# Where the overflow table of the first expert mixture is built: beside the experts, or inside a loop that runs when rows overflow

## The chip, the cores and the metric

The kernel runs on one core of one Trainium2 chip. The metric is device time in microseconds (us) for one execution. [...]

## The reference

The program computes an attention without softmax, then two mixtures of experts, over N = 4608 rows of 512 numbers.

```python
def _attn_ref(q, k, v, g_norm):
    kv = np.einsum('bhsd,bhse->bhde', k, v)
    out = np.einsum('bhsd,bhde->bhse', q, kv)
    rms = np.sqrt(np.mean(out * out, axis=-1, keepdims=True) + 1e-06)
    return out / rms * g_norm

def _moe_ref(x, w_gate, w_output_gate, w1, w2):        # first mixture, 8 experts
    logits = x @ w_gate
    e_idx = np.argmax(logits, axis=1)
    ...
    for e in range(E):
        mask = e_idx == e
        h = np.maximum(x[mask] @ w1[e], 0.0)           # 512 -> 1024
        ye = h @ w2[e]                                 # 1024 -> 512
        out[mask] = gate_w[mask, None] * eom[mask, e, None] * ye
```

The first mixture sends each row to the expert with its largest logit, with no limit on how many rows an expert gets. The second mixture assigns rows greedily with a limit of 576 rows for each expert, and computes the same kind of feed-forward with its own weights.

## The kernel before

Products are done in three passes of a high and a low part (names ending in h and l), so that a result has nearly full fp32 precision. Names: `ph` is the first product's PSUM, `hh` and `hl` the high and low part of its relu, `py` the second product's PSUM, `y` the scaled result, `raw` a weight as loaded, `w1h`, `w1l`, `w2h`, `w2l` its parts, `xg` gathered rows, `sg` their scale, `pt` transposes.

The first mixture's rows are sorted into experts by tables of indices. `experts()` runs over the eight experts, p = 0 to 7, in an order sorted by size, with room for CAPS[p] rows each (672, 704, 672, 640, 608, 608, 576, 544). An expert is eight blocks of `ffn1` (PE products `ph`, ACT `hh`, DVE `hl`), with the splitting of its second weights in blocks 0 to 3 and gathers of the next expert's rows (POOL's indirect DMAs into `xg` and `sg`) in blocks 4 to 7. Then come the rest of the gathers. Behind these, at what is called the boundary here, stands `next(ovf, None)`: one step of `overflow_tables()`. After that the second products of this expert are made tile by tile (PE `py`, ACT `y`, POOL scatters into `x_rows`, DVE logits of the second mixture, scattered by POOL into `l_rows`), beside the splitting of the next expert's first weights (ACT, and POOL's DMAs `w1l`) and the transposes of its gathered rows.

Rows that find no room in their expert go into an overflow table `ovt` in DRAM, in groups of 128. `overflow_tables()` is a generator. In its first step, after expert 0, it fills `ovt` with N by a DMA (L842), counts the groups into `left`, and computes for each row the place in the table (`ri`) and the row's number (`ti`). Each of the six later steps, after experts 1 to 6, issues six scatters of `ti` into `ovt`, each after a small memset of `gap`: 36 in all. After the experts, `left` is read (L1091) and a loop (L1092) runs `spare()` for each group, which reads `ovt`, and gathers, multiplies and scatters. `left` is zero where no row overflows.

The order of PE, DVE, ACT and POOL is written by hand: instructions stand in their lists as the Python code issues them (`manual_schedule`). Nearly all operations pass through one helper, so that they carry its line, L94.

Of the kernel before, what the change touches and what calls it, by code (L numbers as in the profile page):

```python
# [29 lines left out]
N = B * S  # L30
DM = H * D
E = 8
FF = 1024
NT = N // 128
# [21 lines left out]
NOV = 36  # L56
# [43 lines left out]
def moe_chain_kernel(ctx, tc, q, k, v, g_norm, wg1, wog1, w1a, w2a, wg2, w1b, w2b, out, dbg=None):  # L100
    nc = tc.nc
    V = Meter(nc.vector, 150, 1.04)
    A = Meter(nc.scalar, 40, 0.9)
    G = Meter(nc.gpsimd, 70, 2.18)
# [3 lines left out]
    def T(pool, shape, dt, name, **kw):  # L108
        return pool.tile(shape, dt, name=name, **kw)
# [3 lines left out]
    def dram(name, shape, dt=F32):  # L113
        return dbg[name] if name in dbg else tc.dram_tile(shape, dt, name=name)
# [40 lines left out]
    def floor_div(dst, src, n):  # L155

        V.tensor_scalar(dst, src, 1.0 / n, 0.5 / n - 0.5, op0=OP.mult, op1=OP.add)
        V.tensor_scalar(dst, dst, MAGIC, MAGIC, op0=OP.add, op1=OP.subtract)
# [16 lines left out]
    rank_k = T(keep, [128, NT], F32, "rank_k")  # L175
    eid_k = T(keep, [128, NT], F32, "eid_k")
    oneh_k = T(keep, [128, NT, E], BF, "oneh_k")
    cacc = T(keep, [128, E], BF, "cacc")
    V.memset(cacc, 0.0)
    code = T(keep, [128, NT], F32, "code")  # L180
# [6 lines left out]
    cap_e = T(keep, [128, E], F32, "cap_e")  # L187
# [33 lines left out]
    with ExitStack() as at:  # L221
# [243 lines left out]
        with tc.manual_schedule(engines={ENG.PE, ENG.Activation, ENG.DVE, ENG.Pool}):  # L465
# [72 lines left out]
            for t in range(NT):  # L538
                feed(2)
                r, i = divmod(t, TR)  # L540
# [63 lines left out]
        with tc.tile_pool(name="fin", bufs=1) as fin:  # L604
# [14 lines left out]
            def places(src):  # L619
# [20 lines left out]
                            op=OP.is_equal)  # L640
# [109 lines left out]
    with ExitStack() as m1:  # L750
        m1p = m1.enter_context(tc.tile_pool(name="m1p", bufs=1))
# [20 lines left out]
        gap1 = T(spp, [128, 1], F32, "gap1")  # L772
# [13 lines left out]
        def run(k_):  # L786
            for s_ in told:
                s_()
            told.clear()
            while pieces and k_:  # L790
                k_ -= 1
                f_, last_ = pieces.pop(0)
                f_()
                if last_:
                    told.append(last_)
# [35 lines left out]


        ovt = dram("ovt", [NOV * 128 + N, 1], I32)
        left = T(m1p, [128, 1], I32, "left")
        et = [T(m1p, [128, NOV + 1], I32, f"et{i}") for i in range(2)]
        sfc = T(m1p, [128, 1], F32, "sfc")

        def overflow_tables():
            ov = m1.enter_context(tc.tile_pool(name="ov", bufs=1))
            fill = T(ov, [128, NOV], I32, "fill")  # L840
            V.memset(fill, N)
            nc.gpsimd.dma_start(ovt[:NOV * 128, :].rearrange("(p c) o -> p (c o)", p=128), fill)  # L842
            ne = T(ov, [128, E], F32, "ne")
            V.tensor_sub(ne, cnt, cap_e)
            V.tensor_scalar(ne, ne, 0.0, 127.0, op0=OP.max, op1=OP.add)
            te = T(ov, [128, E], F32, "te")
            floor_div(te, ne, 128)
            inc = T(ov, [128, E], F32, "inc")
            onef = T(ov, [128, E], F32, "onef")
            V.memset(onef, 1.0)  # L850
            V.tensor_tensor_scan(inc, onef, te, 0.0, op0=OP.mult, op1=OP.add)
            V.tensor_copy(left, inc[:, E - 1:])
            cmp = T(ov, [128, NOV + 1, E], F32, "cmp", tag="cmp")
            V.tensor_tensor(cmp, lane_f[:, :NOV + 1, None].to_broadcast([128, NOV + 1, E]),
                            inc[:, None, :].to_broadcast([128, NOV + 1, E]), op=OP.is_ge)
            etf = T(ov, [128, NOV + 1], F32, "etf")
            V.tensor_reduce(out=etf, in_=cmp, axis=AX.X, op=OP.add)
            V.tensor_scalar(et[0], etf, float(E - 1), None, op0=OP.min)
            V.tensor_sub(inc, inc, te)
            of = T(ov, [128, NT, E], F32, "of", tag="cmp")  # L860
            rel = T(ov, [128, NT], F32, "rel")
            row = T(ov, [128, NT], F32, "row")
            V.tensor_mul(of, oneh_k, cap_e[:, None, :].to_broadcast([128, NT, E]))
            V.tensor_reduce(out=rel, in_=of, axis=AX.X, op=OP.add)
            V.tensor_sub(rel, rank_k, rel)
            V.tensor_mul(of, oneh_k, inc[:, None, :].to_broadcast([128, NT, E]))
            V.tensor_reduce(out=row, in_=of, axis=AX.X, op=OP.add)
            isv = T(ov, [128, NT], F32, "isv")
            V.tensor_scalar(isv, rel, 0.0, None, op0=OP.is_ge)
            V.scalar_tensor_tensor(row, row, 128.0, rel, op0=OP.mult, op1=OP.add)  # L870
            dr = T(ov, [128, NT], F32, "dr")
            V.tensor_scalar(dr, code, float(NOV * 128 - 128), None, op0=OP.add)
            V.tensor_sub(row, row, dr)
            V.tensor_mul(row, row, isv)
            ri = T(ov, [128, NT], I32, "ri")
            V.tensor_add(ri, row, dr)
            ti = T(ov, [128, NT], I32, "ti")
            V.tensor_scalar(ti, code, -128.0, None, op0=OP.add)
            V.tensor_scalar(sfc, pid, float(NST * 128), None, op0=OP.add)
            prev = []  # L880
            for c in range(NT):
                if c % 6 == 0:
                    yield
                G.memset(gap1, 0.0)
                st = G.indirect_dma_start(out=ovt, out_offset=bass.IndirectOffsetOnAxis(ap=ri[:, c:c + 1], axis=0),
                                          in_=ti[:, c:c + 1], in_offset=None)
                for o in prev:
                    tc.declare_no_dep(st.ins, o.ins, reason="each scatter writes rows of its own")
                prev.append(st)

        def spare(row0):
            it = T(spp, [128, 1], I32, "it")
# [83 lines left out]
        def tiles(p):  # L976
            return [min(128, CAPS[p] - t * 128) for t in range(-(-CAPS[p] // 128))]

        def load1(p):

            if p:
                EM[p] = nc.sync.value_load(eix[0:1, p:p + 1], min_val=0, max_val=E - 1)
                w1_load(w1a[bass.ds(EM[p], 1)].rearrange("o d f -> (o d) f"), p)
# [56 lines left out]
            V.memset(ones36, 1.0)  # L1040

        late = later()
        ovf = overflow_tables()

        def experts():
            for p in range(E):
                m = CAPS[p]
                nxt_ = tiles(p + 1) if p + 1 < E else []
                if nxt_:
                    load1(p + 1)  # L1050
                for f in range(FC):
                    mm, relu, low = ffn1(f, m // 2)
                    low()
                    next(late, None)
                    run(L1)
                    if (p, f) == (0, 0):
                        nc.scalar.dma_start(wg2b.rearrange("p e d -> p (e d)"),
                                            bass.AP(tensor=wg2_t.tensor, offset=wg2_t.offset, ap=[[0, 128], [1, E * DM]]))
                    if 0 < m % 128 <= 64:
                        G.tensor_copy(hh[f][:, m:m + m % 128], hl[f][:, m - m % 128:m])  # L1060
                    if f < FC // 2:
                        w2_split(p, f)
                    elif f - FC // 2 < len(nxt_):
                        gather((p + 1) * TS + f - FC // 2)
                for t in range(FC // 2, len(nxt_)):
                    gather((p + 1) * TS + t)
                next(ovf, None)
                own = tiles(p)
                for t in range(max(len(own), len(nxt_))):
                    if nxt_:  # L1070
                        for c in range(2 * t, min(2 * t + 2, KC)):
                            w1_split(p + 1, c)
                    if t < len(nxt_):
                        rows_t(XG[(p + 1) * TS + t][0], t * 128, nxt_[t], gcol2)
                    run(L2 if nxt_ else E)
                    if t < len(own):
                        n, s_ = own[t], p * TS + t
                        py = ffn2_half(t * 128, n) if n <= 64 else ffn2(t * 128, n)
                        if not nxt_ and t == len(own) - 1:
                            run(len(pieces))  # L1080
                        emit_rows(py, XG.pop(s_)[1], idx_s[:, s_:s_ + 1], n, fold=(n <= 64), end=(p == E - 1 and t == len(own) - 1))
                if nxt_:
                    load2(p + 1)
            run(len(pieces))
            run(0)
            for _ in ovf:
                pass

        with tc.manual_schedule(engines={mybir.EngineType[n] for n in "PE,DVE,Activation,Pool".split(",")}):
            experts()  # L1090
        n_left = nc.values_load(left[0:1, 0:1], min_val=0, max_val=NOV)  # L1091
        with tc.For_i(0, n_left, 1) as i:  # L1092
            spare(bass.ds(i * 128, 128))


    rt2 = ctx.enter_context(tc.tile_pool(name="rt2", bufs=1))
# [7 lines left out]
    own = T(rt2, [CG * E, CG, KT], F32, "own")  # L1104
# [259 lines left out]
    cols, rows, row_t = [], [], [0.0]  # L1364
# [176 lines left out]
```

## Time and profile before

| | us |
|---|---|
| median of 3 timed runs (1285.24 to 1288.03) | 1285.33 |
| profiled execution | 1290.72 |
| span of its trace | 1289.1 |
| PE busy | 1122.4 |
| DVE busy | 784.0 |
| POOL busy | 538.1 |
| ACT busy | 513.4 |

The span runs from the first to the last instruction of one profiled execution. In the rows, PEclk is the share of full speed that was granted to TensorE, `[a <-b]` behind a row is how long its engine had been idle before it and what ended that, "issue" means that the profile shows nothing that it waited for, and "remote" that the releaser is not one of the recorded instructions. Times inside rows are us from the start of the span.

### The profile page before, as it was taken

The numbers are of one execution on the slowest core, as the hardware profiler recorded it, in microseconds if no ns is written. First come the engines' busy times: TensorE is split into PE (matmuls) and PEld (weight loads), VectorE is DVE, ScalarE is ACT, GpSimd is POOL, SyncE is SP. The second block draws the span as 40 slices with busy tenths as digits, with TensorE's granted clock in tenths as the row PEclk, the third lists the DMA queues.
The fourth block names the chain that finished last, engine by engine and source line by source line (L and its number), as shares of the span: only waits on it lengthen the run. The fifth ranks groups of instructions, "written<-read, shape, count | busy, mean of one in ns | idle before, by whom it ended". The sixth has DMA issues, their size and how long they took to land.

```text
span 1289.1 us, 22024 instructions
## 1 busy us (share of the span) xinstructions
PE 1122.4 (87%) x8112; PEld 966.8 (75%) x8112; DVE 784.0 (61%) x2280; ACT 513.4 (40%) x752; POOL 538.1 (42%) x776
## 2 busy tenths in 40 slices
PE   7988388999999897979898349898999998999898
PEld 5877277797979695959687339696878786889696
DVE  2698864857675554728287567676767775771110
ACT  3766543252534344434441033343434343344441
POOL 0545626466765554555743021414142324244221
PEclk8999679999999898979899559999999998999899
DMA  8986674667666665646660073838484948287641
GB/s 278 351 292 221 188 226 135 174 174 179 176 172 175 164 176 144 183 113 172 146 150 34 9 218 81 264 71 242 94 251 84 258 80 247 56 215 218 183 87 37
DMA packets 81022, 216.44 MB, mean 168 GB/s; under 512 B 15208, under 2 KB 15352, under 8 KB 80784
## 3 DMA queue, kind: packets, MB, share of 16 engines
q0 software_dynamic: 37776, 117.23, 40.0%
q1 hardware_dynamic: 41328, 93.03, 20.2%
q10 hardware_dynamic: 1808, 4.75, 1.2%
q8 instruction: 65, 1.06, 0.3%
q14 instruction: 45, 0.37, 0.1%
HBM read 118.46 MB, written 29.40 MB: 115 GB/s over the span
## 4 chain that ended last, share of the span: by engine, by line
PE 62%; DVE 11%; DMA 9%; issue 7%; POOL 4%; ACT 4%; another core or an unknown queue 3%; SPq 0%; POOLq 0%; DVEq 0%; ACTq 0%
PE ph L94 30%; PE py L94 23%; PE pt L94 6%; DMA xg<-x_rows,ix 4%; PE po L94 2%; DMA l_rows<-l,idx_s 2%; PE PB L94 1%; POOL sg L94 1%; DMA w1l<-raw 1%; DVE ms L94 1%; DMA xg<-x_rows,idx_g 1%; DVE scr L94 1%; DVE ol L94 1%; DVE xl__2419 L94 1%
## 5 line engine op out<-in xcount | busy, mean ns | idle before, releaser
L94 PE MATMUL py<-w2h,hh 128*128 128x512 f32 (+2 forms) x664 | 272.4, 410 | 16.7 <-ACT hh L94 8.9
L94 PE MATMUL py<-w2l,hh 128*128 128x512 f32 (+3 forms) x664 | 267.3, 405 | 6.5 <-issue 6.3
L94 DVE SCALAR_TENSOR_TENSOR scr<-y,wg2b 128x512 f32<-128x512 f32 (+3 forms) x336 | 231.6, 689 | 14.0 <-ACT y L94 4.7
L94 PE MATMUL py<-w2h,hl 128*128 128x512 f32 (+1 forms) x560 | 227.2, 406 | 10.7 <-issue 10.4
L94 PE MATMUL ph<-xh,w1h 128*128 128x288 f32 (+5 forms) x1024 | 230.0, 306 | 2.8 <-ACT xh L94 2.3
L94 PE MATMUL ph<-xl__2419,w1h 128*128 128x288 f32 (+5 forms) x1024 | 229.4, 305 | 2.0 <-DVE xl__2419 L94 2.0
L94 PE MATMUL ph<-xh,w1l 128*128 128x288 f32 (+5 forms) x1024 | 228.6, 305 | 0.0
L94 ACT ACTIVATE hh<-ph 128x576 fp32r<-128x576 f32 (+5 forms) x128 | 86.2, 674 | 275.5 <-PE ph L94 220.2
L94 DVE SCALAR_TENSOR_TENSOR hl<-ph,hh 128x576 fp32r<-128x576 f32 (+5 forms) x128 | 99.8, 780 | 150.9 <-ACT hh L94 142.2
L94 PEld LDWEIGHTS ph<-xh,w1h 128*128 128x128 f32 x1024 | 169.6, 190 | 6.0 <-ACT xh L94 3.2
L94 PEld LDWEIGHTS ph<-xl__2419,w1h 128*128 128x128 f32 x1024 | 168.4, 190 | 3.3 <-DVE xl__2419 L94 2.2
L94 PEld LDWEIGHTS ph<-xh,w1l 128*128 128x128 f32 x1024 | 168.8, 190 | 0.9 <-DMA w1l<-raw 0.2
L94 PEld LDWEIGHTS py<-w2h,hh 128*128 128x128 f32 (+2 forms) x664 | 127.5, 192 | 51.0 <-ACT hh L94 11.3
L94 PEld LDWEIGHTS py<-w2l,hh 128*128 128x128 f32 (+3 forms) x664 | 122.4, 184 | 34.4 <-issue 7.6
L94 PEld LDWEIGHTS py<-w2h,hl 128*128 128x128 f32 (+1 forms) x560 | 108.7, 194 | 38.3 <-issue 14.8
L94 POOL DMA_DIRECT2D w2l<-raw x64 | 57.6, 901 | 132.3 <-ACT w2l L94 124.2
L94 POOL CAST hh<-hl 128x64 fp32r<-128x64 f32 (+1 forms) x104 | 51.6, 496 | 123.2 <-DVE hl L94 120.0
L94 POOL DMA_DIRECT2D w1l<-raw x64 | 57.9, 1023 | 105.2 <-ACT w1l L94 62.7
L94 PE MATMUL pt<-identf,xg 128*128 128x128 f32 (+3 forms) x332 | 59.6, 312 | 43.2 <-DMA xg<-x_rows,ix 18.2
L94 POOL DMA_INDIRECT out_dram<-y,ix x40 | 41.1, 1027 | 133.7 <-ACT y L94 92.0
L94 PEld LDWEIGHTS pt<-identf,xg 128*128 128x128 f32 (+3 forms) x332 | 44.5, 163 | 62.6 <-DMA xg<-x_rows,ix 20.4
L94 POOL DMA_INDIRECT x_rows<-y,idx_s x43 | 48.8, 1136 | 93.4 <-ACT y L94 86.3
(286 smaller groups left out, 1635.9 us busy)
## 6 DMA issues: line engine op xcount, KB each, us to landing
raw<-in_moe_w_dram SPq DMA_DIRECT2D x123, 512.0 KB
w1l<-raw POOLq DMA_DIRECT2D x64, 512.0 KB
w2l<-raw POOLq DMA_DIRECT2D x64, 512.0 KB
kt<-in_k_dram SPq DMA_DIRECT2D x32, 288.0 KB
vt<-in_v_dram SPq DMA_DIRECT2D x32, 288.0 KB
qt<-in_q_dram SPq DMA_DIRECT2D x16, 576.0 KB
x_rows<-x POOLq DMA_DIRECT2D x36, 256.0 KB
raw<-in_moe_w_dram ACTq DMA_DIRECT2D x5, 512.0 KB
```

Source lines behind the costliest of these rows:

```text
L94: return f(*a, **kw)
```

## The change

The table of overflow rows is no longer built beside the experts. `overflow_count()` runs once, after expert 0: it computes the counts and writes them to `left`, which has a second column now, min(count, 1). All else (the fill, the places, the 36 scatters) is `overflow_table()`, called inside a loop of zero or one rounds after the experts (L1089 and L1090 in the new kernel); the loop over `spare()` stands inside that loop (L1092 and L1093). The memsets of `gap` ahead of the scatters are gone.

```diff
-        left = T(m1p, [128, 1], I32, "left")
+        left = T(m1p, [128, 2], I32, "left")
...
+        inc = T(m1p, [128, E], F32, "inc")
...
-        def overflow_tables():
+        def overflow_count():
...
-            V.memset(fill, N)
-            nc.gpsimd.dma_start(ovt[:NOV * 128, :].rearrange("(p c) o -> p (c o)", p=128), fill)
...
-            V.tensor_copy(left, inc[:, E - 1:])
+            V.tensor_copy(left[:, 0:1], inc[:, E - 1:])
+            V.tensor_scalar(left[:, 1:2], inc[:, E - 1:], 1.0, None, op0=OP.min)
...
-            prev = []
-            for c in range(NT):
-                if c % 6 == 0:
-                    yield
-                G.memset(gap1, 0.0)
-                st = G.indirect_dma_start(out=ovt, out_offset=bass.IndirectOffsetOnAxis(ap=ri[:, c:c + 1], axis=0),
-                                          in_=ti[:, c:c + 1], in_offset=None)
-                for o in prev:
-                    tc.declare_no_dep(st.ins, o.ins, reason="each scatter writes rows of its own")
-                prev.append(st)
+        def overflow_table():
+
+            with tc.tile_pool(name="ovx", bufs=1) as ov:
+                fill = T(ov, [128, NOV], I32, "fill")
+                V.memset(fill, N)
+                nc.gpsimd.dma_start(ovt[:NOV * 128, :].rearrange("(p c) o -> p (c o)", p=128), fill)
+                of = T(ov, [128, NT, E], F32, "of")
...
+                ti = T(ov, [128, NT], I32, "ti")
+                V.tensor_scalar(ti, code, -128.0, None, op0=OP.add)
+                for c in range(NT):
+                    G.indirect_dma_start(out=ovt, out_offset=bass.IndirectOffsetOnAxis(ap=ri[:, c:c + 1], axis=0),
+                                         in_=ti[:, c:c + 1], in_offset=None)
...
-                next(ovf, None)
+                if not p:
+                    overflow_count()
...
-            for _ in ovf:
-                pass
...
-        n_left = nc.values_load(left[0:1, 0:1], min_val=0, max_val=NOV)
-        with tc.For_i(0, n_left, 1) as i:
-            spare(bass.ds(i * 128, 128))
+        n_any = nc.values_load(left[0:1, 1:2], min_val=0, max_val=1)
+        with tc.For_i(0, n_any, 1):
+            overflow_table()
+            n_left = nc.values_load(left[0:1, 0:1], min_val=0, max_val=NOV)
+            with tc.For_i(0, n_left, 1) as i:
+                spare(bass.ds(i * 128, 128))
```

On POOL, at the boundary after expert 4, the list before has this from the last gathers (`xg`, `sg`) to the low parts of the next expert's first weights (`w1l`); the pair of memset and scatter stands there six times:

```order
L94 DMA xg<-x_rows,idx_g 128x512
L94 DMA sg<-sg_rows,idx_w 128x1
L94 MEMSET gap_2489 128x1
L94 DMA ovt<-ti,ri 9216x1
...
L94 DMA w1l_134<-raw 128x1024
L94 DMA w1l_135<-raw 128x1024
L94 MEMSET gap_2489 128x1
L94 DMA x_rows<-y,idx_s 15360x512
```

The same place in the new list:

```order
L94 DMA xg<-x_rows,idx_g 128x512
L94 DMA sg<-sg_rows,idx_w 128x1
L94 DMA w1l_134<-raw 128x1024
L94 DMA w1l_135<-raw 128x1024
L94 MEMSET gap_2489 128x1
L94 DMA x_rows<-y,idx_s 15360x512
```

The `w1l` DMAs and the scatters of `y` into `x_rows` now stand directly behind the gathers. The same holds at the other five boundaries.

On PE, at the end of the experts, the difference is this: the last products of the first mixture (`pt`, with `yT`), the reading of `left` and the branches over the loops, and then the first product of the loop's body. The rows with a - are of before.

```order
 L94 MATMUL pt<-wg2s,yT 32x8 x4
-L1091 TENSOR_LOAD left
-L1092 COMPARE_AND_BRANCH
-L1092 UNCONDITIONAL_BRANCH x2
-L1536 BRANCH_PREFETCH_HINT
+L1089 TENSOR_LOAD left
+L1090 COMPARE_AND_BRANCH
+L1090 UNCONDITIONAL_BRANCH x2
+L1537 BRANCH_PREFETCH_HINT
+L1092 TENSOR_LOAD left
+L1093 COMPARE_AND_BRANCH
```

A second load and branch stands inside the first loop, ahead of the spare tiles' products.

## Rows read from the trace of the kernel before

**Rows 1.** The page: engines' busy time and share of the span; the chain.

```profile
PE 1122.4 (87%) x8112; PEld 966.8 (75%) x8112; DVE 784.0 (61%) x2280; ACT 513.4 (40%) x752; POOL 538.1 (42%) x776
...
PE 62%; DVE 11%; DMA 9%; issue 7%; POOL 4%; ACT 4%; another core or an unknown queue 3%; SPq 0%; POOLq 0%; DVEq 0%; ACTq 0%
```

**Rows 2.** Table of stretches, from first scatters to dense products: engines' busy time.

```profile
core 0: us, PE busy (x) PEld busy (x) DVE busy (x) ACT busy (x) POOL busy (x), PEclk, DMA share, GB/s
290.30:302.00 11.70, 9.69 (x47) 7.73 (x46) 5.15 (x14) 2.84 (x5) 10.37 (x17) 1.00 0.28 52
353.50:365.00 11.50, 9.34 (x41) 7.29 (x40) 4.86 (x13) 6.32 (x8) 10.16 (x17) 0.97 0.23 47
418.00:429.70 11.70, 5.66 (x18) 3.45 (x19) 1.57 (x2) 5.87 (x8) 8.77 (x15) 0.83 0.36 55
483.40:497.00 13.60, 5.19 (x16) 3.08 (x15) 0.79 (x1) 3.18 (x4) 6.90 (x14) 0.64 0.04 11
551.90:565.50 13.60, 6.53 (x17) 3.56 (x17) 0.79 (x1) 3.02 (x4) 6.74 (x14) 0.63 0.05 12
623.60:636.00 12.40, 7.91 (x28) 5.28 (x27) 0.00 (x0) 2.10 (x3) 9.71 (x17) 0.78 0.39 59
sum 74.50, PE 44.32 PEld 30.40 DVE 13.17 ACT 23.32 POOL 52.64; mean PE 7.39 PEld 5.07 DVE 2.20 ACT 3.89 POOL 8.77
```

**Rows 3.** The waits: engine and tile, releaser, total us, times, longest.

```profile
ACT hh L94 <- remote: 37.9, 3, 15.0
...
PE py L94 <- issue: 23.3, 21, 1.7
```

**Rows 4.** Timeline of ACT, expert 4: start and duration in us.

```profile
478.22 0.68 ACT L94 ACTIVATE hh<-ph 128x608 fp32r<-128x608 f32 x1 [5.35 <-PE ph L94]
493.82 0.68 ACT L94 ACTIVATE hh<-ph 128x608 fp32r<-128x608 f32 x1 [14.92 <-remote]
```

**Rows 5.** Timeline of PE, expert 4.

```profile
478.32 0.44 PE L94 MATMUL ph<-xh,w1l 128*128 128x304 f32 x2
...
483.17 0.40 PE L94 MATMUL py<-w2l,hh 128*128 128x512 f32 x1 [0.99 <-issue]
...
494.55 0.79 PE L94 MATMUL py<-w2h,hh 128*128 128x512 f32 x1 [5.83 <-ACT hh L94]
```

**Rows 6.** Timeline of POOL, expert 4.

```profile
482.48 0.96 POOL L94 DMA_INDIRECT sg<-sg_rows,idx_w  x1 [0.30 <-issue]
...
490.16 0.97 POOL L94 DMA_INDIRECT ovt<-ti,ri  x1 [0.19 <-issue]
496.69 1.00 POOL L94 DMA_DIRECT2D w1l<-raw  x1 [5.56 <-ACT w1l L94]
```

**Rows 7.** Table of stretches, expert 4: gathers, then scatters.

```profile
469.60:483.40 13.80, 12.80 (x84) 12.07 (x84) 4.96 (x11) 1.35 (x2) 10.86 (x12) 1.00 0.87 255
483.40:491.10 7.70, 2.74 (x8) 1.15 (x6) 0.00 (x0) 0.00 (x0) 6.56 (x13) 0.75 0.07 19
```

**Rows 8.** Table of stretches with second products, without scatters of ti.

```profile
364.00:381.00 17.00, 17.00 (x73) 13.58 (x72) 14.57 (x39) 3.93 (x7) 8.90 (x14) 0.90 1.08 257
234.15:246.00 11.85, 11.85 (x58) 9.52 (x57) 11.43 (x32) 2.55 (x5) 4.74 (x8) 1.00 0.96 301
```

**Rows 9.** Timeline of ACT, experts 3 and 6.

```profile
417.56 0.70 ACT L94 ACTIVATE hh<-ph 128x640 fp32r<-128x640 f32 x1 [7.96 <-remote]
...
633.90 0.69 ACT L94 ACTIVATE y<-py,sg 128x512 f32<-128x512 f32 x1 [12.21 <-issue]
```

**Rows 10.** Timeline of PE, boundary after expert 0.

```profile
224.66 0.39 PE L94 MATMUL py<-w2h,hl 128*128 128x512 f32 x1 [1.51 <-issue]
226.76 0.39 PE L94 MATMUL py<-w2h,hh 128*128 128x512 f32 x1 [1.71 <-issue]
```

**Rows 11.** Timeline around the end of the first mixture.

```profile
713.42 0.86 POOL L94 DMA_INDIRECT l_rows<-l,idx_s  x1 [0.91 <-DVE l L94]
...
717.06 0.22 DVE L94 TENSOR_SCALAR wide<-lane_f 65x120 fp32r<-65x120 f32 x1 [3.92 <-issue]
```

More of the change, by code (lines that the diff above doesn't have):

```diff
@@ L833, in moe_chain_kernel @@
         ovt = dram("ovt", [NOV * 128 + N, 1], I32)
-        left = T(m1p, [128, 1], I32, "left")
+        left = T(m1p, [128, 2], I32, "left")
         et = [T(m1p, [128, NOV + 1], I32, f"et{i}") for i in range(2)]
         sfc = T(m1p, [128, 1], F32, "sfc")
-        def overflow_tables():
+        inc = T(m1p, [128, E], F32, "inc")
+        def overflow_count():
             ov = m1.enter_context(tc.tile_pool(name="ov", bufs=1))
-            fill = T(ov, [128, NOV], I32, "fill")
-            V.memset(fill, N)
-            nc.gpsimd.dma_start(ovt[:NOV * 128, :].rearrange("(p c) o -> p (c o)", p=128), fill)
             ne = T(ov, [128, E], F32, "ne")
@@ L847, in overflow_tables @@
             floor_div(te, ne, 128)
-            inc = T(ov, [128, E], F32, "inc")
             onef = T(ov, [128, E], F32, "onef")
@@ L851, in overflow_tables @@
             V.tensor_tensor_scan(inc, onef, te, 0.0, op0=OP.mult, op1=OP.add)
-            V.tensor_copy(left, inc[:, E - 1:])
-            cmp = T(ov, [128, NOV + 1, E], F32, "cmp", tag="cmp")
+            V.tensor_copy(left[:, 0:1], inc[:, E - 1:])
+            V.tensor_scalar(left[:, 1:2], inc[:, E - 1:], 1.0, None, op0=OP.min)
+            cmp = T(ov, [128, NOV + 1, E], F32, "cmp")
             V.tensor_tensor(cmp, lane_f[:, :NOV + 1, None].to_broadcast([128, NOV + 1, E]),
@@ L859, in overflow_tables @@
             V.tensor_sub(inc, inc, te)
[L860 to L877, printed above, removed]
@@ L878, in overflow_tables @@
-            V.tensor_scalar(ti, code, -128.0, None, op0=OP.add)
-            V.tensor_scalar(sfc, pid, float(NST * 128), None, op0=OP.add)
-            prev = []
-            for c in range(NT):
-                if c % 6 == 0:
-                    yield
-                G.memset(gap1, 0.0)
-                st = G.indirect_dma_start(out=ovt, out_offset=bass.IndirectOffsetOnAxis(ap=ri[:, c:c + 1], axis=0),
-                                          in_=ti[:, c:c + 1], in_offset=None)
-                for o in prev:
-                    tc.declare_no_dep(st.ins, o.ins, reason="each scatter writes rows of its own")
-                prev.append(st)
+            V.tensor_scalar(sfc, pid, float(NST * 128), None, op0=OP.add)
@@ new lines, in overflow_table @@
+        def overflow_table():
[4 more added lines that the diff above has]
+                of = T(ov, [128, NT, E], F32, "of")
+                rel = T(ov, [128, NT], F32, "rel")
+                row = T(ov, [128, NT], F32, "row")
+                V.tensor_mul(of, oneh_k, cap_e[:, None, :].to_broadcast([128, NT, E]))
+                V.tensor_reduce(out=rel, in_=of, axis=AX.X, op=OP.add)
+                V.tensor_sub(rel, rank_k, rel)
+                V.tensor_mul(of, oneh_k, inc[:, None, :].to_broadcast([128, NT, E]))
+                V.tensor_reduce(out=row, in_=of, axis=AX.X, op=OP.add)
+                isv = T(ov, [128, NT], F32, "isv")
+                V.tensor_scalar(isv, rel, 0.0, None, op0=OP.is_ge)
+                V.scalar_tensor_tensor(row, row, 128.0, rel, op0=OP.mult, op1=OP.add)
+                dr = T(ov, [128, NT], F32, "dr")
+                V.tensor_scalar(dr, code, float(NOV * 128 - 128), None, op0=OP.add)
+                V.tensor_sub(row, row, dr)
+                V.tensor_mul(row, row, isv)
+                ri = T(ov, [128, NT], I32, "ri")
+                V.tensor_add(ri, row, dr)
+                ti = T(ov, [128, NT], I32, "ti")
[3 more added lines that the diff above has]
+                                         in_=ti[:, c:c + 1], in_offset=None)
@@ L1042, in moe_chain_kernel @@
         late = later()
-        ovf = overflow_tables()
         def experts():
```

## The prediction

> **What bounds the kernel now.** I read the page's engine lines and chain first, then the waits, then tables of stretches, and last the timelines of single boundaries. The page says that TensorE is busy for 1122.4 of 1289.1 us and heads the chain with 62%, while POOL is busy for only 538.1 us, and 4% of the chain is POOL's [rows 1]. By these shares alone, POOL work that is taken out looks like work taken from beside the products. So the question is whether there are stretches where TensorE is not the bound, and whether the 36 scatters stand in them.
>
> They do. The first mixture has eight experts, and at the boundary after each of experts 1 to 6 POOL issues six scatters in a row. I cut out the stretch from each first scatter to where the products run densely again: six stretches, 74.50 us together, in which TensorE is busy for 44.32 us [rows 2]. Two of them, after experts 4 and 5, are the worst: 5.19 and 6.53 us of products in 13.60 us each. VectorE, ScalarE and the DMA engines are idle there as well (0.79 us, 3.18 us and a DMA share of 0.04 in the fourth stretch), so neither arithmetic nor bytes bound it.
>
> The list of waits names what the engines stand for. ACT's `hh` (the relu that empties the first product's PSUM) waited 37.9 us in three times for a "remote" releaser, and PE's `py` waited 23.3 us in 21 times for "issue", which is nothing that the profile shows [rows 3]. In the timeline of expert 4 the relu before the last begins at 478.22 and the last one at 493.82, after 14.92 us idle [rows 4], although PE began the last product that it reads at 478.32 [rows 5]. The relu needs no more than that product and a buffer, and both were there. Meanwhile POOL gathers up to 483.44, then scatters without a pause until 491.13 (490.16 + 0.97), and its next instruction waits for ACT until 496.69 [rows 6]. The relu starts 2.7 us after the last scatter was done, and PE's `py`, which reads its result, restarts at 494.55 after 5.83 us of idling [rows 5]. My reading: while POOL issues indirect DMAs back to back, word of a finished product reaches the other engines, and PE's own next instruction, late, and the debt is paid off only after the run of them ends.
>
> **What the change takes away.** Of each boundary six scatters and six small memsets go: 7.70 us with the gaps between them, 6.56 us of it busy [rows 7]. POOL as such loses 6 x 7.70 = 46 us, but POOL was no bound: the gain is what TensorE and ACT get back in the six stretches, and this has to be worked out from the products.
>
> The six stretches hold 47 + 41 + 18 + 16 + 17 + 28 = 167 products [rows 2]. Two stretches without such a run of scatters give what these would take: 58 in 11.85 us (0.204 us each, at a granted clock of 1.00) and 73 in 17.00 us (0.233 us, at 0.90) [rows 8]. So 167 of them need 34.1 to 38.9 us, and 74.50 less that, 35.6 to 40.4 us, is lost now. I take 39, nearer the row at the full clock, since a stretch with dense products should be granted it, where these six got 0.63 to 1.00 [rows 2].
>
> Not all of it comes back. The gathers of the next expert's rows stay, and they are instructions of the same kind on the same engine. In the 13.80 us of gathers ahead of expert 4's scatters PE is still busy for 12.80 us [rows 7]: PE works from what was ready before, but the debt builds. With the scatters gone the run ends at 483.44 instead of 491.13. If the last relu again comes 2.7 us after the end, it starts near 486.1, and PE, whose first gap ends at 483.17 [rows 5], waits some 3 us instead of the 8.4 us that the stretch now lacks (13.60 - 5.19). I leave 3 us each after experts 4 and 5. After expert 3 the relu had been released already by 417.56, before its stretch of scatters begins at 418.00, after 7.96 us idle [rows 2, 9]: what follows there is the scatters' alone, and I leave 1 us. After experts 1, 2 and 6 I leave 0.5 us each; the ACT wait of 12.21 us at expert 6 ends in the scatters' shadow [rows 9]. Together 8.5 us stay, and 39 - 8.5 = 30.5 us are gained.
>
> Bounds of what stays: nothing, or what the boundary after expert 0 shows. There POOL issues its gathers in a row and no scatter, and PE has two gaps, 1.51 and 1.71 us [rows 10]; 3.2 us at each of six boundaries is 19 us, and the gain is 20.
>
> **The other parts.** The fill DMA and the DVE arithmetic of the table leave the boundary after expert 0, and one DVE operation (the second column of `left`) is added. What waits next at that boundary waits behind gathers on POOL, not for DVE, and DVE is 61% busy [rows 1]; I count 0, with bounds of a few tenths either way, the size of the smallest DVE operation in the rows, 0.22 us [rows 11]. The weights' low parts (`w1l`) and the scatters of `y` move up by 7.7 us on POOL's queue; they wait for ACT, which is itself released earlier, and nothing stands behind them that was not behind the scatters. The DMA share of 0.04 says that there is room for them [rows 2].
>
> At the end of the first mixture the loop over the spare tiles is skipped: DVE idles 3.92 us before its next operation at 717.06 [rows 11], and no gather or product of a spare tile stands between 713.42 and there, so the count is zero and the new outer loop is skipped too. The inner loop's load and branch lie inside the outer one and are jumped over. The skip should cost what it costs now: I count 0, with bounds of 0 and one more such exit, 3.9 us, since the inner loop's instructions now lie between. No part of this was ever beside the products.
>
> **The sum.** The profiled execution took 1290.72 us; 1290.7 - 30.5 = 1260.2. It is 5.4 us above the median of the timed runs, 1285.33, which I take to be the same in both kernels: 1260.2 - 5.4 = 1254.8, said as 1255.
>
> **Rivals.** *The gathers hold PE as well* (17%). What delays the products is then any run of POOL's indirect DMAs, and once the scatters go, the gathers, `w1l` and the `y` scatters close up and make a run almost as bad as before. For it: expert 0's two gaps, and that the relu of expert 3 waited 7.96 us with no scatter yet issued. Against it: PE stays at 12.80 of 13.80 us in the gathers. The time is 1285.3 - 20 = 1265, and up to 1281 if the gathers' debt is worse than at expert 0.
>
> *The stalls are the recorder's* (8%). [...] If the waits were made by it, the timed runs never had them, and stay at 1285. Against it: the profiled execution is only 5.4 us longer than the median, where stalls that only it had would make it some 39 us longer; with those 5.4 us taken from the 39, the gain is still 25 us, 1260. [...]
>
> *Slower by the exit* (4%). The boundaries return nothing, because the `py` products wait there for something that I have not seen, and the exit of two loops takes two of the waits of 3.92 us [rows 11]: 1285.3 + 3.9 = 1289.2 and more. It decides only where the boundaries return less than these 3.9 us. For it: the exit has DVE idle with nothing beside it. Against it: the inner loop is jumped over. That the loop is entered after all would be worse (36 scatters of 1.28 us in line, 46 us), but the trace shows no spare tile, and I give it no share of its own.
>
> *More than I think* (3%): all 40.4 us come back, 1285.3 - 40.4 = 1244.9, and the gather stretches, where PE now lacks 1.00 us of 13.80 [rows 7], gain as well: 1243 or less.
>
> **How the numbers follow.** The forecast, 68%, is 1255, and its own range is 1245 (all of the 40.4 us lost now come back) to 1262 (7 us more: one more exit of 3.9 us, and 3 us of debt above the 8.5). The range to hold the time 8 times in 10 runs from 1243 to 1276: it has the forecast's 68% and most of the first rival, and leaves out the recorder, the exit, and the rival's upper end. Within 0.3% (3.9 us) a measurement of this kernel can't tell a difference: faster by more than that is 68 + 17 + 3 = 88%, no difference 8%, slower 4%.
>
> **What will show it.** In the new profile each of the six boundaries should have the last relu within 3 us of the last gather's end, no ACT `hh` wait on "remote" of 15 us at experts 4 and 5, the `py` waits for "issue" down from 23.3 to under 8 us, and the PE gaps of expert 0's boundary as they are. DVE's wait before `wide` should stay at 3.9 us. The forecast is wrong if the 15 us waits move to the gathers or to the `y` scatters, if PE has the same idle time under another name, or if the profile improves by 30 us and the timed runs do not.

## The result and the profile after

In the rows, PE is TensorE and PEld its weight loads, DVE is VectorE, ACT is ScalarE, POOL is GpSimd and SP is SyncE. In the trace of the kernel before, DMAs are issued by POOL (453), SP (211) and ACT (9).

The changed kernel takes 1253.8 us (median; 1248.57 to 1260.54), the kernel before beside it 1286.68 us (1285.24 to 1291.02). The ratio is 0.9729 with a 95% interval of 0.9689 to 0.9769. The forecast was 1255.

The profiled execution of the changed kernel took 1248.57 us, 42.2 us less than the profiled one of before. The page, answering to [rows 1]; its first line is the span:

```profile
span 1246.9 us, 21951 instructions
...
PE 1102.8 (88%) x8112; PEld 956.7 (77%) x8112; DVE 782.2 (63%) x2268; ACT 513.1 (41%) x752; POOL 500.8 (40%) x703
...
PE 62%; DVE 13%; DMA 10%; issue 7%; ACT 3%; POOL 3%; another core or an unknown queue 1%; SPq 0%; POOLq 0%; DVEq 0%; ACTq 0%
```

Busy shares hardly moved. The gain shows when the span is cut by experts, from one expert's first product to the next one's. First before, then after: experts 1 to 6 together, and expert 4 alone (columns as in [rows 2]).

```profile
249.61:651.68 402.07, 369.56 (x2022) 322.78 (x2021) 231.48 (x585) 164.72 (x210) 235.34 (x332) 0.95 0.65 164
451.94:520.35 68.41, 59.00 (x333) 51.40 (x332) 34.97 (x88) 26.58 (x34) 35.82 (x50) 0.93 0.62 162
```

```profile
244.35:603.49 359.14, 354.18 (x2022) 315.69 (x2021) 232.89 (x590) 164.29 (x210) 196.43 (x261) 1.00 0.71 184
430.97:490.23 59.26, 56.85 (x333) 50.40 (x332) 37.01 (x94) 26.57 (x34) 29.22 (x38) 1.00 0.71 187
```

The same 2022 products take 42.9 us less. The rows split this: PE stands still for 32.5 us before (402.07 - 369.56) and for 5.0 us after, which is 27.5 us, and the same products are busy for 15.4 us less, at a mean granted clock of 1.00 where it was 0.95. So about a third of the gain is in shorter products: in before the clock was down to 0.64 and 0.63 in the stretches where PE stood most, after experts 4 and 5 [rows 2]. The rest of the span moved by -5.3 us ahead of expert 1, where runs of one kernel differ by as much (expert 1 begins at 249.61 us here and at 244.22 in the trace of before in sitting 2), by +0.5 us in the second mixture, and by two losses: +1.4 us from expert 7's first product to the second mixture's (+3.3 in sitting 2 below), and +4.2 us at the very end.

The waits, answering to [rows 3]:

```profile
ACT hh L94 <- remote: 21.8, 3, 8.0
...
DVE wide L94 <- issue: 7.0, 1, 7.0
...
PE py L94 <- issue: 5.7, 7, 1.1
```

The late relus of experts 3 to 5 are still there but shorter (21.8 for 37.9 us), and PE's `py` waits for "issue" are 5.7 instead of 23.3 us. A new name is in the list: `wide`, the first operation of DVE behind the loop, waits 7.0 us, where it waited 3.92 [rows 11]. Expert 4 again, answering to [rows 4 to 6], in timelines of ACT, PE and POOL:

```profile
464.48 0.68 ACT L94 ACTIVATE hh<-ph 128x608 fp32r<-128x608 f32 x1 [6.55 <-remote]
```

```profile
462.19 0.39 PE L94 MATMUL py<-w2l,hh 128*128 128x512 f32 x1 [1.14 <-issue]
464.31 0.39 PE L94 MATMUL py<-w2h,hl 128*128 128x512 f32 x1 [1.05 <-issue]
```

```profile
461.49 0.96 POOL L94 DMA_INDIRECT sg<-sg_rows,idx_w  x1 [0.30 <-issue]
467.36 1.01 POOL L94 DMA_DIRECT2D w1l<-raw  x1 [4.91 <-ACT w1l L94]
```

POOL's run of indirect DMAs ends at 462.45 and the relu follows 2.0 us later (2.7 us were expected); PE loses two gaps of 1.1 us, where before it lacked 8.4 us in the stretch from 483.40 to 497.00 [rows 2].

Of the signs that were named, the 15 us waits of `hh` are gone (the longest is 8.0), and the `py` waits are under 8 us. At expert 5 the last relu comes 2.1 us after the last gather, as at expert 4. In experts 1, 2 and 6 it comes 7 to 9 us ahead of the last gather in both kernels, so this sign tells nothing there. Two signs failed: `wide` waits 7.0 instead of 3.9 us, and the PE gaps of expert 0's boundary did not stay as they were (0.80 and 1.07 us for 1.51 and 1.71).

The trace also holds records of semaphores that the engines raise; I take such a record as the word that an instruction is finished, since those of ACT and DVE stand within 0.02 us of such an end (below). At expert 4 of the kernel before, the five products that end from 475.43 to 478.77 us have theirs at 478.20, 479.64, 483.19, 488.14 and 493.80 us (paired in their order), and ACT's last two relus begin 0.02 us after the first and the last of these. So the word of the last product is 15.0 us late. In experts 1 to 6, of the 144 records of PE that the trace holds, 36 stand more than 0.05 us behind the nearest end of a product that signals; all 180 of ACT and all 303 of DVE stand within 0.02 us of theirs. Of these three engines it is TensorE's word alone that is late. In the changed kernel 27 of 146 are, by up to 6.3 us.

### The profile page after: what moved, and what is told of

It is laid out like the page before. It is cut to its first block, busy times and chain, and to the rows that moved or that the text cites. A ratio compares the mean times of both kernels' runs of the same rounds, so it can differ in the third digit from the quotient of the medians.

```text
span 1246.9 us, 21951 instructions
## 1 busy us (share of the span) xinstructions
PE 1102.8 (88%) x8112; PEld 956.7 (77%) x8112; DVE 782.2 (63%) x2268; ACT 513.1 (41%) x752; POOL 500.8 (40%) x703
## 4 chain that ended last, share of the span: by engine, by line
PE 62%; DVE 13%; DMA 10%; issue 7%; ACT 3%; POOL 3%; another core or an unknown queue 1%; SPq 0%; POOLq 0%; DVEq 0%; ACTq 0%
PE ph L94 31%; PE py L94 23%; PE pt L94 6%; DMA xg<-x_rows,ix 4%; DVE scr L94 3%; DMA qt<-in_q_dram 1%; PE po L94 1%; PE PB L94 1%; DMA xg<-x_rows,idx_g 1%; DMA vt<-in_v_dram 1%; DVE ms L94 1%; DVE hl L94 1%; DMA w1l<-raw 1%; DVE ol L94 1%
## 5 line engine op out<-in xcount | busy, mean ns | idle before, releaser
L94 PE MATMUL py<-w2h,hh 128*128 128x512 f32 (+2 forms) x664 | 267.5, 403 | 1.8 <-issue 1.5
L94 PE MATMUL py<-w2l,hh 128*128 128x512 f32 (+3 forms) x664 | 263.1, 399 | 2.4 <-issue 2.4
L94 PE MATMUL py<-w2h,hl 128*128 128x512 f32 (+1 forms) x560 | 222.7, 398 | 2.1 <-issue 1.8
L94 PEld LDWEIGHTS py<-w2h,hh 128*128 128x128 f32 (+2 forms) x664 | 124.9, 188 | 33.2 <-issue 3.5
L94 PEld LDWEIGHTS py<-w2h,hl 128*128 128x128 f32 (+1 forms) x560 | 106.1, 189 | 25.4 <-issue 1.7
L94 ACT ACTIVATE w1h<-raw 128x1024 fp32r<-128x1024 f32 x64 | 67.1, 1049 | 51.4 <-DMA raw<-in_moe_w_dram 51.4
```

Source lines behind the costliest of these rows:

```text
L94: return f(*a, **kw)
```

## The experiments

Kernels sent together ran on one chip, with the kernel before beside them; I call that a sitting. The kernel before took 1234.9 us in sitting 1 (chip 6), 1291.0 in 2 (chip 0), 1277.7 in 3 and 1278.6 in 4 (chip 6), and 1234.0 in 5 (chip 13). All its runs in a sitting lie within 11 us of the median, so these are two conditions of the same program, 43 to 57 us apart, and a chip number was seen in both. I call what sets the longer one apart the lateness; the first comparison (1286.68) had it too.

**Sitting 1: what in the scatters costs.** Four variants of the kernel before.

```diff
-                G.memset(gap1, 0.0)
-                st = G.indirect_dma_start(out=ovt, ...)
+                for _ in range(4):
+                    G.memset(junk, 0.0)
```

> The kernel before, with each of the 36 scatters and its small memset replaced by four memsets of 128x256 numbers on POOL, so that POOL is busy as long (about 1.25 us for 1.28 us) at the same places, but issues no DMA there; the overflow table stays empty of rows. Experts 1 to 6 (from the first product of expert 1 to that of expert 7) took 402.1 us in the trace of before and 359.1 us in that of after. Theory (runs of POOL's indirect DMAs delay the word of finished products): 360 +- 6 us here, last relu of expert 4 within 3 us of the last gather, execution about 1247 to 1255 us. Rival (POOL being occupied for 7.7 us holds up the w1l DMAs and y scatters behind it, and these the products): 395 to 405 us as before, execution about 1285 us.

```diff
-                st = G.indirect_dma_start(out=ovt, ...)
+                st = G.dma_start(ovt[NOV * 128 + c * 128:NOV * 128 + (c + 1) * 128, :], ti[:, c:c + 1])
```

> The kernel before, with each of the 36 indirect scatters replaced by a plain DMA that POOL issues at the same place: the same column of 128 numbers of 4 bytes, to 128 neighbouring rows of the table (the memset ahead of it stays; the table's rows are at fixed places and not where rows overflow). Theory in the form 'indirect DMAs alone do it': experts 1 to 6 take 360 +- 6 us. In the form 'any DMA that POOL issues in a run does it': 390 to 402 us. Rival (the 128 small packets of 4 bytes, or the recording of them, do it): as before, 395 to 405 us.

```diff
-                if c % 6 == 0:
-                    yield
+                yield
...
+                    if p and f < 6:
+                        next(ovf, None)
                     if f < FC // 2:
                         w2_split(p, f)
...
-                next(ovf, None)
+                if not p:
+                    next(ovf, None)
```

> The kernel before, with the 36 scatters all kept, but one at a time: in experts 1 to 6 one in each of the blocks 0 to 5 of the first product, in place of six in a row at the boundary. Theory (it is the run that builds a debt; single indirect DMAs cost the products nothing): experts 1 to 6 take 359 to 366 us, execution 1247 to 1260 us. Rival (each scatter costs its share, 43 us over 36 = 1.2 us, wherever it stands): 395 to 402 us, execution 1280 us or more.

```diff
-            for c in range(NT):
+            for c in range(0, NT, 2):
                 if c % 6 == 0:
                     yield
```

> The kernel before with every second scatter left out: three in a row at each of six boundaries, 18 in all (the other rows are not written to the table). If the price goes by the scatter: experts 1 to 6 take half of the 43 us between before and after, about 381 us. Theory (a debt that builds during the run, and that the products feel only once what was ready before is used up): the first scatters are the cheaper ones, so less than half, 365 to 379 us. Rival (a run costs a fixed sum whatever its length): 390 us or more.

Measured against 1234.86 us of before: memsets 1238.15 us (ratio 1.0008 to 1.0042), plain DMAs 1230.83 (0.9957 to 1.0002), half the scatters 1235.83 (0.9986 to 1.0027). None of the expectations met this: here the scatters cost nothing to begin with, and the three runs do not tell the theories apart. They do show something else. With half the scatters, experts 1 to 6 and expert 4 read:

```profile
243.90:595.48 351.58, 351.58 (x2021) 316.05 (x2020) 234.99 (x597) 165.25 (x210) 214.79 (x298) 1.00 0.75 187
429.19:485.39 56.20, 56.20 (x333) 50.48 (x332) 36.75 (x94) 26.79 (x34) 32.16 (x44) 1.00 0.78 199
```

PE never stands, and all 159 of its words in experts 1 to 6 come within 0.02 us. And this although POOL issues its gathers and then scatters in one run, as its timeline shows, with ACT's last relus of expert 4 under it:

```profile
460.30 0.95 POOL L94 DMA_INDIRECT sg<-sg_rows,idx_w  x1 [0.30 <-issue]
461.24 0.12 POOL L94 MEMSET gap<- 128x1 f32 x1
461.56 0.99 POOL L94 DMA_INDIRECT ovt<-ti,ri  x1 [0.19 <-issue]
```

```profile
452.72 0.68 ACT L94 ACTIVATE hh<-ph 128x608 fp32r<-128x608 f32 x1 [2.60 <-PE ph L94]
456.06 0.68 ACT L94 ACTIVATE hh<-ph 128x608 fp32r<-128x608 f32 x1 [2.66 <-PE ph L94]
```

The relus come every 3.3 us, each released by its product. The kernel before itself took 1234.86 us here, so the lateness is no property of the program; a trace of it was not taken without lateness. With plain DMAs experts 1 to 6 take 351.58 us as well, with memsets 351.84. So 351.6 us is what they take without lateness, and this is the floor for what follows.

The spread scatters are another matter: 1289.88 us (1.0408 to 1.0497), experts 1 to 6 in 410.7 us. The theory was wrong. The rival's 1280 us or more was met, but not its cause, since scatters in a row cost nothing that the times show in this sitting (1234.86 us with six, 1235.83 with three). The waits of that kernel name it:

```profile
PE pt L94 <- DMA xg<-x_rows,idx_g: 48.2, 8, 8.6
```

The scatters now stand ahead of the gathers in POOL's list, and PE waits for the gathered rows. The last gather of an expert ends 4.4 to 9.7 us later after the expert's first product than with half the scatters, and a gather of `xg` takes 7.3 us (median) from its issue to its landing, for 4.3. That is POOL's order, with no late word: all 159 records of PE in these experts stand within 0.02 us.

**Sitting 2: before and after again, and one loop in place of two.**

> The kernel before, unchanged, for its trace on the chip on which four variants gave 1228 to 1290 us while before itself gave 1234.9 us there instead of 1286.7. Theory (the delay of TensorE's word of finished products belongs to the chip or to the loading of the program, and was absent there): about 1235 us on such a chip, experts 1 to 6 in 351 +- 4 us as in the variants there (351.1 to 351.8 us), no ACT hh wait on remote; or, on a chip as the first, about 1286 us and 402 us. Rival (something in the variants' session alone, such as a run of short length): a time between, 1250 to 1275 us.

> The changed kernel, unchanged, beside before on the same chip. Theory (the 43 us that experts 1 to 6 gave back were the delayed words alone): where before takes about 1235 us, no gain at the boundaries, and one more exit of the loop, 3.1 us: 1236 to 1240 us, a ratio of 1.000 to 1.004; where before takes about 1286 us, a ratio near 0.973. Rival (the scatters cost products also without that delay): a ratio of 0.985 or less on both kinds of chip.

```diff
-        n_any = nc.values_load(left[0:1, 1:2], min_val=0, max_val=1)
-        with tc.For_i(0, n_any, 1):
-            overflow_table()
-            n_left = ...
-            with tc.For_i(0, n_left, 1) as i:
-                spare(bass.ds(i * 128, 128))
+        n_left = nc.values_load(left[0:1, 0:1], min_val=0, max_val=NOV)
+        with tc.For_i(0, n_left, 1) as i:
+            overflow_table()
+            spare(bass.ds(i * 128, 128))
```

> The changed kernel with one loop in place of two nested ones: the loop over spare tiles runs left times, and each round first builds the overflow table anew and then does its tile. Theory (leaving two nested loops costs one more exit, 7.0 instead of 3.9 us before the operation wide): wide waits 3.9 us again and the time is 3 us under that of after on the same chip. Rival (the 3.1 us lie beside other work, as the wait for l_rows): wide waits less, but the start of the second mixture comes no earlier than in after, 0 us.

The kernel before took 1292.0 us as a variant of itself; beside its 1290.95 us over the whole sitting, after took 1253.22 (ratio 0.9674 to 0.9807) and one loop 1254.2 (0.9661 to 0.9782). Experts 1 to 6 of before, then of after:

```profile
244.22:644.24 400.02, 365.75 (x2022) 321.29 (x2020) 232.40 (x588) 164.74 (x210) 234.82 (x333) 0.95 0.65 166
```

```profile
244.59:607.11 362.52, 355.97 (x2022) 316.67 (x2020) 232.14 (x588) 164.35 (x210) 194.63 (x260) 1.00 0.71 182
```

The first comparison repeats. All intervals of the changed kernel lie under 1, though only that of the first comparison lies wholly under 0.98 (those of sittings 2 to 4 end at 0.981 to 0.982). With one loop, `wide` waits less, but not as little as before:

```profile
677.48 0.22 DVE L94 TENSOR_SCALAR wide<-lane_f 65x120 fp32r<-65x120 f32 x1 [5.36 <-issue]
```

Of the 3.1 us that the exit grew (3.92 to 7.02), 1.7 belong to the second loop; 1.4 stay with one loop around a longer body. The second mixture begins 116.15 us after expert 7's first product with one loop and 117.97 after in the same sitting, so that the rival's 0 us was not met either. The times of the two kernels are not told apart.

**Sitting 3: the question of sitting 1, with the lateness present.**

Memsets stand after experts 1, 3 and 5, plain DMAs after 2, 4 and 6.

```diff
+                if c // 6 % 2 == 0:
+                    for _ in range(4):
+                        G.memset(junk, 0.0)
+                    continue
                 G.memset(gap1, 0.0)
-                st = G.indirect_dma_start(out=ovt, ...)
+                G.dma_start(ovt[NOV * 128 + c * 128:NOV * 128 + (c + 1) * 128, :], ti[:, c:c + 1])
```

> The kernel before, with the 36 scatters replaced in two ways: at the boundaries after experts 1, 3 and 5 by four memsets of 128x256 numbers each on POOL, after experts 2, 4 and 6 by a plain DMA of the same 128 numbers each (the table is not the reference's). On a chip with the delay, as the one of the first and second comparison, experts 3 to 6 took 67.9, 68.4, 70.3 and 61.0 us with the scatters and 59.0, 59.3, 59.3 and 53.9 us without. Theory in the form 'indirect DMAs alone': 3 to 6 as without, within 2 us each. Theory in the form 'any run of DMAs that POOL issues': 3 and 5 as without, 4 and 6 as with. Rival (POOL being occupied): all four as with. On a chip without the delay all four are short whatever stands there: 57.7, 56.2, 56.6 and 53.5 to 53.7 us, and the run tells nothing on this.

> The changed kernel, unchanged, once more, for the chip that comes. On a chip where before takes about 1235 us, theory (the change is worth the delay of TensorE's words and nothing else): 1236 to 1240 us, ratio 1.000 to 1.004, from the 3.1 us of the second loop's exit. Rival (the scatters take products' time also there): ratio 0.985 or less. On a chip where before takes about 1290 us: ratio 0.974 again.

The mixed kernel took 1248.4 us (0.9717 to 0.9827 of before's 1277.69), after 1249.88 (0.9744 to 0.9817). Experts 3, 5 and 6 of the first trace of before (expert 4 is above), then 3 to 6 of the mixed kernel:

```profile
384.02:451.94 67.92, 61.47 (x334) 54.00 (x333) 38.96 (x99) 27.63 (x35) 36.07 (x52) 0.95 0.64 161
520.35:590.63 70.28, 62.29 (x333) 52.77 (x332) 38.28 (x99) 26.58 (x34) 36.28 (x50) 0.90 0.61 157
590.63:651.68 61.05, 56.56 (x326) 49.18 (x325) 31.10 (x78) 26.25 (x34) 38.91 (x56) 0.94 0.70 171
```

```profile
372.15:429.82 57.67, 57.67 (x334) 52.60 (x332) 38.92 (x100) 27.52 (x35) 37.23 (x64) 1.00 0.62 148
429.82:490.37 60.55, 58.98 (x334) 51.52 (x332) 37.08 (x96) 26.59 (x34) 32.80 (x50) 0.97 0.82 222
490.37:549.55 59.18, 57.19 (x333) 50.51 (x332) 35.38 (x90) 26.58 (x34) 37.20 (x62) 1.00 0.68 170
549.55:603.03 53.48, 53.48 (x325) 48.02 (x324) 34.36 (x89) 26.28 (x34) 35.74 (x56) 1.00 0.79 194
```

All four are, within 0.1 us, as in the changed kernel, which has nothing there, over its four traces with the lateness (57.7 to 62.9, 58.8 to 60.5, 59.1 to 59.4, 53.5 to 53.9), and none as with indirect scatters in the two traces of before (67.9 to 68.8, 68.4, 68.2 to 70.3, 61.0 to 62.0). With POOL occupied by memsets (four of 0.312 us for each scatter) experts 3 and 5 took 57.67 and 59.18 us, no more than in after, and with plain DMAs expert 4 took 1 to 2 us more at most (60.55) and expert 6 none (53.48): of the three it is the indirect DMAs that the loss went with. The lateness was there: before took 1277.69 us, and ACT's `hh` still waits 22.0 us for "remote" in the mixed kernel, around the gathers. One reservation: six plain DMAs keep POOL busy for less time (0.579 us each, an indirect one 0.973).

**Sitting 4: the rest at experts 4 and 5.** The kernel with one loop, and gathers begun two blocks sooner.

```diff
-                    elif f - FC // 2 < len(nxt_):
-                        gather((p + 1) * TS + f - FC // 2)
+                    f0 = 2 if p else FC // 2
+                    if f0 <= f < f0 + len(nxt_):
+                        gather((p + 1) * TS + f - f0)
-                for t in range(FC // 2, len(nxt_)):
+                for t in range(FC - f0, len(nxt_)):
...
```

> The changed kernel with the single loop of f_flat, and with the gathers of the next expert's rows begun two blocks sooner in experts 1 to 6 (one pair in each of blocks 2 to 7, none left over for the boundary). Theory (what is left at experts 4 and 5 with the delay, 59.0 and 59.3 us against 56.2 and 56.6 us without it, is the run of gathers across the last blocks): spread out, the delayed words are paid off before the second products need them, experts 4 and 5 take 56 to 57.5 us, and the execution is 4 to 8 us under that of after on the same chip. Rival (the gathers delay the words just as long wherever they stand): 59 us each, within 2 us of after. A second rival (the early gathers stand in front of the w2l DMAs and hold up the weights): blocks 2 to 5 get longer, slower than after. On a chip without the delay: within 3 us of after, from the exit alone.

> The changed kernel, unchanged, to stand beside h_early. With the delay (before at 1278 to 1291 us): ratio 0.973 to 0.978, experts 4 and 5 at 58.8 to 59.4 us. Where before takes about 1235 us: theory (the change is worth the delayed words alone) 1.000 to 1.004; rival 0.985 or less.

1243.41 us (1241.95 to 1245.72) beside after's 1249.45 (1245.41 to 1252.64); against before 0.969 to 0.975, and 0.9725 to 0.9807. Experts 1 to 6 and expert 4 with the early gathers, then of after in the same sitting:

```profile
247.49:599.81 352.32, 352.11 (x2022) 315.87 (x2020) 234.17 (x593) 164.55 (x210) 195.60 (x262) 1.00 0.73 188
433.51:489.71 56.20, 56.20 (x333) 50.49 (x332) 37.95 (x97) 26.58 (x34) 29.81 (x38) 1.00 0.76 197
```

```profile
245.98:605.07 359.09, 355.73 (x2021) 317.07 (x2020) 232.80 (x590) 164.23 (x210) 195.65 (x261) 1.00 0.71 184
431.77:492.25 60.48, 59.15 (x333) 51.56 (x332) 37.52 (x96) 26.57 (x34) 29.35 (x38) 0.97 0.70 183
```

Expert 4 takes exactly what it took without any lateness, and expert 5 does too (56.62 us). After's expert 4 was 60.48 us, 1.1 above what was expected. The gathers still delay words:

```profile
ACT hh L94 <- remote: 17.6, 3, 7.2
```

But PE loses only 0.2 us in 352.32. It is not that the run ends sooner: at expert 4 the gathers end 30.8 us after the expert's first product, for 31.5 in after, while second products run from 27.0. They begin earlier, though, and are spread over 16.5 instead of 13.8 us, and the last relu comes 29.4 us after that first product, for 33.4 in after and 26.9 without lateness. PE does not stand for it, with other second products to do until then. So late words cost PE next to nothing in this trace (0.2 us), since they are in before the products need them. This version is 6.0 us faster than after by the medians, and it beats both kernels, though its range just touches after's.

**Sitting 5: by the number of scatters.**

```diff
+                if c % 6 >= (6, 6, 3, 2, 4, 3)[c // 6]:
+                    continue
                 G.memset(gap1, 0.0)
```

> The kernel before with fewer scatters at some boundaries: 6 after experts 1 and 2, 3 after expert 3, 2 after expert 4, 4 after expert 5, 3 after expert 6 (the other rows are not written to the table). With the delay, experts 3 to 6 take 67.9 to 68.8, 68.4, 68.2 to 70.3 and 61.0 to 62.0 us with six and 57.7 to 62.9, 58.8 to 60.5, 59.2 to 59.4 and 53.5 to 53.9 us with none. If each scatter costs its share: about 64, 62.3, 66 and 57.6 us. Theory (each scatter lengthens a run that already delays words, at expert 4 and 5 from its first one on; at experts 3 and 6, where the words were nearly paid off, the first ones are free): 4 and 5 by the share, 3 and 6 under 61 and 55.5 us. Rival (a run costs a fixed sum): all as with six. Without the delay (before at 1235 us): all short, and the run tells nothing on this.

1236.22 us, before 1234.0 (1.0000 to 1.0032): the lateness was absent, and how the price goes by the number stays open. Experts 1 to 6 took 351.57 us here too.

## Why the prediction was right, and where it was not

**The mechanism.** The prediction read from the waits that words of finished products come late while POOL issues indirect DMAs back to back. The semaphore records show these words and their lateness, up to 15.0 us. Sitting 3 shows that neither POOL's time (57.67 and 59.18 us at experts 3 and 5) nor plain DMAs (60.55 and 53.48 us at experts 4 and 6) do it, and sitting 4 that with the gathers begun sooner and spread wider late words cost PE 0.2 us.

**The size of the gain** was too small: 30.5 us foreseen, 42.9 measured in experts 1 to 6. The floor of 351.6 us splits it. Before lost 402.07 - 351.58 = 50.5 us, after still loses 359.14 - 351.58 = 7.6. What stays was well put (8.5), also by experts: 1.3, 3.1, 2.7 and 0.5 us at experts 3 to 6 against 1, 3, 3 and 0.5. Later traces of after lose 5.1 to 10.9 us, so a hit this close is in part luck. The failed term is the 39 us "lost now". I set before's products beside those of the kernel with half the scatters, one by one: the lag grows by 2.7 us ahead of the six stretches, by 41.9 inside them, and by 5.9 behind them. Inside, the rate at the full clock (40.4) was nearer than the one taken; that dense products should be granted this clock was an estimate, and the rows have both (0.90 with PE busy for 17.00 of 17.00 us [rows 8], 1.00 with 12.80 of 13.80 [rows 7]); the rest lies outside the windows that were cut, above all behind them.

**The exit** was put at 0 with a bound of 3.9 us; it grew by 3.1.

**A term was missing.** At the end of the program the last scatter is issued, and the span closes after it. The last POOL rows of before and after, against spans of 1289.1 and 1246.9 us:

```profile
1284.97 0.91 POOL L94 DMA_INDIRECT out_dram<-y,ix  x1 [3.37 <-DVE y L94]
```

```profile
1238.61 0.91 POOL L94 DMA_INDIRECT out_dram<-y,ix  x1 [3.37 <-DVE y L94]
```

From its end to the end of the span are 3.2 us before and 7.4 us after. This is no chance: it is 3.2 in before again, with the plain DMAs and with the spread scatters, all of which have 36 DMAs to the table on POOL, and 6.9 to 7.5 in every kernel with 24, 18 or none. In the trace's records it is POOL's last long drain that gets longer, 3.5 us in the former and 7.2 to 7.8 in the latter. Why, was not tried.

**The offset** of 5.4 us from profile to median was taken as equal in both kernels. It was not: before's profiled execution lay 4.0 us above its median of 1286.68, after's 5.2 us under its median of 1253.8. In the other sittings with the lateness the timed gain was 37.7, 27.8 and 29.2 us. So 1255 was hit because errors of opposite sign cancelled. The profile came out 12.4 us lower for experts 1 to 6 and 4.8 lower for what varies from run to run (-5.3 and +0.5), and higher by 1.4 and 4.2 for the way to the second mixture and the end; the offset came out 10.6 higher (+5.2 for -5.4). That is 17.2 against 16.2. The range and the sign rest on the mechanism, the last digit doesn't.

**The rivals.** *The gathers hold PE as well* happened only as far as the 7.6 us go. *The stalls are the recorder's* stays open, and the argument against it was void: each timed run comes with a span and a granted clock, so it was recorded too, and the 5.4 us between profile and median say nothing. What the traces add speaks for it in part. In the sittings with lateness they have lost semaphore records: 12151 are left in before, where the kernel with spread scatters, which does the same work, holds 14698 without lateness; of PE's 763 there are 731 to 741. But records are lost also where no time is: in the second mixture before holds 3972 of 4433, only 3 of PE's 350 there are late, and that mixture takes 463 to 468 us in all traces, with the lateness and without. These traces show losses and late words in the same sittings, and not whether one brings the other about. No execution here ran without a recording, so whether the lateness, and with it the gain, is there without one is not shown. *Slower by the exit* had a true core: exit and end cost 3.1 + 4.2 = 7.3 us. Where there is no lateness nothing pays for them, and my estimate for the changed kernel there is at most about 1234 + 7, slower than before. It may be less: the three kernels with the longer end were only 1.0 to 3.3 us slower than before there. The changed kernel did not run in such a sitting. Nothing in the prediction had foreseen that the kernel before itself has two times. What brings the lateness about is not shown.

## What to carry to other kernels

Where an engine waits for "issue" or "remote" and the tensors it needs are done, look at what another engine issues in a row at that time; begin a run of indirect DMAs sooner and spread it, so that late words are in before the products need them (sitting 4: PE lost 0.2 us in experts 1 to 6, where it lost 3.4 in after); but set single ones ahead of gathers only if the gathers can wait (sitting 1: PE waited 48.2 us for gathered rows). Cut the span by repeating pieces of work and set each against the best the same piece ever took: that gives the loss without windows chosen by hand. Time the kernel before in several sittings before a gain of a few per cent is called one, and look at the end of the program too (4.2 us here).

## What the runs showed of the hardware

- The same program took 1234 to 1235 us in two sittings and 1278 to 1291 us in three and the first comparison. 50.5 us (402.07 in the first trace of before, 351.58 in a sitting without the lateness) lie in experts 1 to 6, where TensorE's word of completion came up to 15.0 us late beside runs of POOL's indirect DMAs, while the words of ACT and DVE that were recorded came within 0.02 us.
- Behind loops that are not entered DVE waited for "issue" ahead of `wide`: 3.6 to 4.1 us with one loop around a short body (3.92 in the first trace of before), 5.4 with one around a longer body (5.36 with one loop in sitting 2), 7.0 to 7.5 with two nested ones (7.02 in the first trace of after).
- An indirect DMA of 128 numbers occupied POOL for 0.97 us (median of 36 in the first trace of before), a plain one of the same numbers for 0.58 us (median of 36 in sitting 1).
- POOL's last long drain took 3.5 us in the kernels with 36 DMAs from POOL to the overflow table, and 7.2 to 7.8 us in each kernel with fewer.
